# One float32 product for the router's rows and logits, and pools whose long matmul operands begin at multiples of 512 bytes

## The chip, the core and the metric

The kernel runs on one core of a Trainium2 chip. The metric is the device time of one execution in microseconds (us); three runs of the kernel before gave 4136.3, 4138.6 and 4139.27 us, median 4138.6 us. Engines are named as in the profile: PE (matrix products; PEld is its loading of the stationary operand), ACT, DVE, POOL, and SP, which issues most DMAs. A matmul has a stationary operand (`lhsT`, loaded first) and a moving operand (`rhs`, streamed through).

## The reference

```python
X = rfft(x, axis=1)                                   # x: 8 x 3072 x 256
Yr = Xr @ w_r - Xi @ w_i + b_r;  Yi = Xr @ w_i + Xi @ w_r + b_i
Y = soft_threshold(Yr, 0.01) + 1j * soft_threshold(Yi, 0.01)
x = irfft(Y, n=3072, axis=1).reshape(24576, 256)
h = x @ w_in                                          # 256 x 2048
x = where(h >= 1, h, where(h <= -1, 0, (h + 1)**2 / 4)) @ w_out
logits = x @ w_gate                                   # 256 x 8 experts
e = argmax(logits);  gate = softmax(logits)[e]        # per token
out = gate * (relu(x @ w1[e]) @ w2[e])                # 256 x 1024, 1024 x 256
```

## The kernel before

There are three stages, each bounded by pools of SBUF memory that are opened and closed in turn.

The spectral stage (`spectral`, to about 558 us) does the transform as two small products per batch, mixes with the complex weights (L278), thresholds, and does half of the inverse (L305). The dense stage (`Moe1.run`, about 559 to 2925 us) walks over 48 units of 512 tokens with 16 steps each. A step (u, f) is written out in program order: six products of 512 columns for layer 1 (L664: `win` stationary, `yh` and `yl` moving), the nonlinearity on ACT and DVE (L669 to L671), a split of the result into high and low parts (ACT L678, POOL L679), and six products of 512 columns for layer 2 of the step three back (L689: `wout` stationary, `gh` and `gl` moving). The expert stage (`Moe2.run`, from 2925 us) walks over a list of tiles of 512 ("big", 41 of them), 256 (17) and 128 tokens (4). A big tile has eight steps of six 512-column products (L956: `w1b` stationary, `xh`, `xl` moving) and twelve 256-column products (L987: `hh`, `hl` stationary, `w2b` moving). The weights stand in three buffers each: big tiles alternate between `w1b`/`w2b` 0 and 1, the small tiles use 2 (`buf`).

The products run in float32r on operands split into a high and a low part. A float32r product is one record in the trace. A plain float32 product stands in the trace as two records, called passes here; a transpose is one.

Between the first two stages and the experts lies the router. When the dense stage has finished a unit, `Router.add` copies its output to `xc` (256 channels on partitions by 512 tokens, float32) and queues small jobs; `router.jobs.run(3)` takes three of them, `None` included, per step. Two jobs (`rows`, L515) transpose four 128x128 blocks each, so that tokens stand on partitions; ACT copies them to `rw` (L518). A third (`logits`, L524) makes eight float32 products with only 8 moving columns, the gate weights `wg`, and DVE copies them to `lg` (L526). Every second unit, `route` finds the expert and the gate from `lg`, stores token number and gate in the last two columns of `rw`, writes `rw` to the DRAM array `xs`, and works out each token's slot; the slots are written one indirect DMA per step from POOL's queue (`place`, L595). The experts later fetch slots (L877), rows of `xs` (L913) and weights (L877) with indirect DMAs of the same queue and transpose the rows back (L923).

SBUF tiles follow each other in a pool, each rounded to 32 bytes, so a tile's start follows from the sizes of all before it. In the built program of the kernel before, starts modulo 512 bytes are: `win`, `wout` and `yh`, `yl` 480; `gh`, `gl` 352; `w1b0`, `w2b0` 128; `w1b1`, `w1b2`, `w2b1`, `w2b2` and the experts' `xh`, `xl` 352; `hh`, `hl` 480; in the spectral stage `wh`, `wl`, `i1h`, `i1l` 256, and the moving `zh`, `zl` 384. L278's stationary operands start at many different offsets, because they are windows of 194 columns.

Of the kernel before, what the change touches and what calls it, by code (L numbers as in the profile page):

```python
# [10 lines left out]
F32 = mybir.dt.float32  # L11
# [29 lines left out]
XW = D + 2  # L41
# [134 lines left out]
def spectral(tc, nc, a, P, A_dr, B_dr, NB, side, room):  # L176
# [11 lines left out]
    f1 = const.tile([96, 96], F32, name="f1")  # L188
    f1h = const.tile([96, 96], F32R, name="f1h")
    f1l = const.tile([96, 96], F32R, name="f1l")  # L190
# [5 lines left out]
    bias = const.tile([128, 3, D], F32, name="bias")  # L196

# [290 lines left out]
class Router:  # L488


    def __init__(self, tc, nc, a, K, sb, xs_dr, slots):
        self.tc, self.nc, self.K, self.sb, self.xs_dr, self.slots = tc, nc, K, sb, xs_dr, slots
        self.wg = sb.tile([128, 2, NE], F32, name="wg", bufs=1)
        self.open = {}
        self.jobs, self.moves, self.hold = Jobs(), deque(), False
        nc.gpsimd.dma_start(self.wg, a["moe2_w_gate"].rearrange("(c p) e -> p c e", p=128))

    def add(self, u, n, psum):

        sb, nc = self.sb, self.nc  # L500
        k = u % n
        if k == 0:
            self.open[u] = (sb.tile([128, 8, NE], F32, tag="lg", name="lg"),
                            sb.tile([128, 8, XW], F32, tag="rw", name="rw"))
        lg, rw = self.open[u - k]
        xc = sb.tile([128, 2, TT], F32, tag="xc", name="xc")
        nc.scalar.activation(xc, psum, AF.Copy)

        def rows(h):

            p = self.rank_tile()
            for c in range(2):
                for dc in range(2):
                    o = (2 * h + c) * 128
                    nc.tensor.transpose(p[:, (2 * c + dc) * 128:(2 * c + dc + 1) * 128], xc[:, dc, o:o + 128],  # L515
                                        self.K["ident"])
            t = 4 * k + 2 * h
            nc.scalar.activation(rw[:, t:t + 2, 0:D], p.rearrange("p (c d) -> p c d", c=2), AF.Copy)  # L518

        def logits():  # L520
            p = self.rank_tile()
            for c in range(4):
                for dc in range(2):
                    nc.tensor.matmul(p[:, c * NE:(c + 1) * NE], lhsT=xc[:, dc, c * 128:(c + 1) * 128],  # L524
                                     rhs=self.wg[:, dc, :], start=(c == 0 and dc == 0), stop=(c == 3 and dc == 1))
            nc.vector.tensor_copy(out=lg[:, 4 * k:4 * k + 4, :],  # L526
                                  in_=p[:, 0:4 * NE].rearrange("p (c e) -> p c e", c=4))
        self.jobs.add(None, None, None, partial(rows, 0), None, None, partial(rows, 1), None, None, logits, None, None)
        if k == n - 1:
            self.open.pop(u - k)  # L530
            self.jobs.add(self.route(4 * (u - k), 4 * n, lg, rw))

    def route(self, c0, T, lg, rw):
        tc, sb, K = self.tc, self.sb, self.K
        v, sc, pe, gp, sp = self.nc.vector, self.nc.scalar, self.nc.tensor, self.nc.gpsimd, self.nc.sync
        lg, rw = lg[:, 0:T, :], rw[:, 0:T, :]
# [35 lines left out]
        v.reciprocal(out=rw[:, :, D + 1], in_=sm)  # L572
        v.tensor_copy(out=rw[:, :, D].bitcast(I32), in_=ids[:, 0, c0:c0 + T])
# [146 lines left out]
class Moe2:  # L720


    def __init__(self, tc, nc, K, sb, xs_dr, slots, w_dr, out):
        self.tc, self.nc, self.K, self.pre, self.xs_dr, self.slots = tc, nc, K, sb, xs_dr, slots
        self.w_dr, self.out = w_dr, out
        self.w1b = [sb.tile([128, 2, 2, FE], F32R, name="w1b0")]
# [95 lines left out]
    def listing(self, sb, tag, n, num, start, per, back, sure):  # L822
# [5 lines left out]
        def t2(name, dt=F32):  # L828
            return sb.tile([128, n], dt, name=f"{name}_{tag}", bufs=1)
        tt, et, cs, wf, si, wi = t2("tt"), t2("et"), t2("cs"), t2("wf"), t2("si", I32), t2("wi", I32)  # L830
        b3 = sb.tile([128, n, NE], F32, name=f"b3_{tag}", bufs=1)
        last = sb.tile([128, 1], F32, name=f"last_{tag}", bufs=1)
# [85 lines left out]
    def turn(self, t, dc):  # L918
        r, C = self.xr[t], self.chunks(t)
        n = C * 128  # L920
        p = self.ps.tile([128, 512], F32, tag="px", name="px")
        for c in range(C):
            self.nc.tensor.transpose(p[:, c * 128:(c + 1) * 128], r[:, c, dc * 128:(dc + 1) * 128], self.K["ident"])  # L923
        if dc == 0:
            self.xt[t] = (self.sb.tile([128, 2, 512], F32R, tag="xh", name="xh"),
                          self.sb.tile([128, 2, 512], F32R, tag="xl", name="xl"))
        xh, xl = self.xt[t]
        v = self.nc.vector
        self.nc.scalar.activation(xh[:, dc, :n], p[:, :n], AF.Copy)  # L929
        v.tensor_tensor(out=xl[:, dc, :n], in0=p[:, :n], in1=xh[:, dc, :n].bitcast(F32), op=ALU.subtract)  # L930
        if dc == 1:
            o = self.sb.tile([128, 4], I32, tag="oi", name="oi", bufs=4)
            v.tensor_tensor(out=o[:, :C], in0=r[:, :C, D].bitcast(I32), in1=self.ix.pop(t)[2], op=ALU.add)
            self.oi[t] = o
# [57 lines left out]
    def finish(self, t):  # L992
# [4 lines left out]
        for c in range(C):  # L997
            w = r[:, c, D + 1:D + 2]
# [63 lines left out]
def body(tc, a, out, NB=8):  # L1062
# [39 lines left out]
    with tc.manual_schedule():  # L1102
# [10 lines left out]
        def side(s, pool):  # L1113
# [87 lines left out]
```

## Time and profile before

| | |
|---|---|
| median of three runs | 4138.6 us |
| profiled execution: its own time | 4134.41 us |
| its span of engine work | 4132.6 us |
| PE busy | 4100.5 us, 99% |
| DVE, ACT, POOL busy | 53%, 44%, 43% |
| granted TensorE clock, mean | 0.997 of 2.4 GHz |

A PE group's busy time counts matmuls that overlap each other in the pipeline, so the mean of one (401 ns for 512 columns) is longer than the distance between two starts. What a matmul costs on a busy PE is read from that distance, in the timeline.

### The profile page before, as it was taken

What the parts mean: (1) busy time and instruction counts of PE and PEld (TensorE: products, weight loads), DVE (VectorE), ACT (ScalarE), POOL (GpSimd) and SP (SyncE); (2) the same over time, 40 slices, a digit from 0 to 9 for tenths busy, and PEclk for the clock granted to TensorE, in tenths of its full rate; (3) what the DMA queues carried; (4) which work ended last, traced back from release to release, by engine and by line L of the source; (5) the groups of instructions that cost most, each with busy time, mean ns of one, the idle gap of its engine ahead of it and who ended that gap; (6) DMA issues with size and microseconds to landing.
All of it is one profiled execution on the core that took longest, in us unless ns stands there. A gap on an engine that the chain in (4) does not pass through costs nothing.

```text
span 4132.6 us, 61734 instructions
## 1 busy us (share of the span) xinstructions
PE 4100.5 (99%) x23596; PEld 3564.1 (86%) x23596; DVE 2196.6 (53%) x4082; ACT 1817.9 (44%) x3266; POOL 1794.2 (43%) x1590
## 2 busy tenths in 40 slices
PE   8999999999999999999999999999999999999999
PEld 6999988888888888888888888888889899999998
DVE  6999965555555555555555555555533333333333
ACT  5666544444444444444444444444322322232232
POOL 1000024444445454444454555556455545445453
PEclk9999999999999999999999999999999999999999
DMA  8767512211211221222112210002223321113222
GB/s 263 220 212 215 174 49 48 57 48 45 54 50 50 48 52 47 51 49 49 50 50 56 58 31 22 22 21 62 68 88 108 102 85 46 48 43 130 89 82 74
DMA packets 204344, 321.79 MB, mean 78 GB/s; under 512 B 43284, under 2 KB 167090, under 8 KB 200976
## 3 DMA queue, kind: packets, MB, share of 16 engines
q1 hardware_dynamic: 157968, 213.09, 18.6%
q0 software_dynamic: 46080, 104.76, 8.2%
q8 instruction: 185, 3.03, 0.4%
q14 instruction: 111, 0.91, 0.1%
HBM read 392.10 MB, written 136.61 MB: 128 GB/s over the span
## 4 chain that ended last, share of the span: by engine, by line
PE 97%; DMA 1%; DVE 1%; issue 1%; POOL 0%; ACT 0%; SPq 0%; POOLq 0%; ACTq 0%; DVEq 0%
PE po L689 26%; PE pl L664 26%; PE po L987 13%; PE pl L956 13%; PE pmx L278 6%; PE pi L649 3%; PE pf L225 2%; PE prk L524 2%; PE pf L246 2%; PE pi L305 2%; PE px L923 1%; PE prk L515 1%; DMA A<-ao 1%; DMA xr<-xs,gi 0%; DMA at<-A 0%
## 5 line engine op out<-in xcount | busy, mean ns | idle before, releaser
L679 POOL TENSOR_TENSOR gl<-g,gh 128x512 fp32r<-128x512 f32 x768 | 992.6, 1292 | 1125.4 <-ACT gh L678 1078.9
L670 DVE SCALAR_TENSOR_TENSOR q<-q 128x512 f32<-128x512 f32 x768 | 532.3, 693 | 864.5 <-ACT q L669 862.5
L669 ACT ACTIVATE q<-pl,half 128x512 f32<-128x512 f32 x768 | 527.7, 687 | 1027.8 <-PE pl L664 1027.3
L664 PE MATMUL pl<-yh,win 128*128 128x512 f32 x3072 | 857.8, 401 | 0.9 <-DVE g L671 0.9
L689 PE MATMUL po<-gh,wout 128*128 128x512 f32 x3072 | 835.4, 393 | 0.0
L689 PEld LDWEIGHTS po<-gh,wout 128*128 128x128 f32 x3072 | 576.2, 188 | 125.7
L664 PEld LDWEIGHTS pl<-yh,win 128*128 128x128 f32 x3072 | 556.4, 188 | 113.7 <-DVE g L671 1.8
L961 DVE SCALAR_TENSOR_TENSOR hl<-pl,hh 128x512 fp32r<-128x512 f32 x396 | 273.7, 691 | 576.9 <-ACT hh L960 574.9
L671 DVE TENSOR_TENSOR g<-pl,q 128x512 f32<-128x512 f32 x768 | 531.3, 692 | 83.2 <-DVE q L670 4.6
L960 ACT ACTIVATE hh<-pl 128x512 fp32r<-128x512 f32 x396 | 237.3, 599 | 639.8 <-PE pl L956 625.5
L689 PE MATMUL po<-gl,wout 128*128 128x512 f32 x1536 | 483.6, 395 | 0.0
L678 ACT ACTIVATE gh<-g 128x512 fp32r<-128x512 f32 x768 | 477.2, 621 | 4.2 <-DVE g L671 4.2
L664 PE MATMUL pl<-yl,win 128*128 128x512 f32 x1536 | 474.3, 390 | 0.0
L987 PEld LDWEIGHTS po<-w2b,hh 128*128 128x128 f32 x3232 | 434.9, 188 | 29.1
L956 PE MATMUL pl<-xh,w1b 128*128 128x512 f32 (+1 forms) x1856 | 454.8, 367 | 0.7 <-ACT xh L929 0.7
L987 PE MATMUL po<-w2b,hh 128*128 128x256 f32 x3232 | 449.4, 281 | 0.0
L689 PEld LDWEIGHTS po<-gl,wout 128*128 128x128 f32 x1536 | 288.3, 188 | 69.9
L664 PEld LDWEIGHTS pl<-yl,win 128*128 128x128 f32 x1536 | 288.4, 188 | 65.1
L956 PEld LDWEIGHTS pl<-xh,w1b 128*128 128x128 f32 x1856 | 297.8, 189 | 30.5 <-ACT xh L929 1.3
L1005 POOL DMA_INDIRECT out<-y,oi x202 | 205.2, 1016 | 210.7 <-ACT y L1000 162.7
L956 PE MATMUL pl<-xl,w1b 128*128 128x512 f32 (+1 forms) x928 | 260.0, 361 | 0.0
L987 PE MATMUL po<-w2b,hl 128*128 128x256 f32 x1616 | 258.3, 282 | 0.8 <-DVE hl L961 0.8
(260 smaller groups left out, 4760.1 us busy)
## 6 DMA issues: line engine op xcount, KB each, us to landing
xs<-rw SPq DMA_DIRECT2D x24, 1032.0 KB, 6.5
A<-ao SPq DMA_DIRECT2D x64, 384.0 KB, 4.2
at<-A SPq DMA_DIRECT2D x96, 256.0 KB, 3.7
B<-bo SPq DMA_DIRECT2D x96, 256.0 KB, 2.7
xt<-in_x SPq DMA_DIRECT2D x56, 384.0 KB, 4.8
ws<-in_moe_w SPq DMA_DIRECT2D x128, 128.0 KB, 3.3
w_dr<-wsh SPq DMA_DIRECT2D x128, 128.0 KB, 1.8
w_dr<-wsl SPq DMA_DIRECT2D x128, 128.0 KB, 2.5
```

What stands on the lines that cost most here:

```text
L278: pe.matmul(p[:, gi, :], lhsT=l, rhs=r, start=(i == 0), stop=(i == 11))
L664: self.nc.tensor.matmul(p, lhsT=w[:, kc, f * 128:(f + 1) * 128], rhs=y[:, kc, :], start=(i == 0), stop=(i == 5))
L669: self.nc.scalar.activation(q, p, AF.Relu, bias=self.K["half"], scale=0.5)
L670: v.scalar_tensor_tensor(out=q, in0=q, scalar=1.0, in1=q, op0=ALU.min, op1=ALU.mult)
L671: v.tensor_tensor(out=g, in0=p, in1=q, op=ALU.max)
L678: self.nc.scalar.activation(gh, g, AF.Copy)
L679: self.nc.gpsimd.tensor_tensor(out=gl, in0=g, in1=gh.bitcast(F32), op=ALU.subtract)
L689: self.nc.tensor.matmul(self.po[u][:, dc, :], lhsT=w[:, f, dc * 128:(dc + 1) * 128], rhs=g, start=(f == 0 and i == 0), stop=(f == 15 and i ...
L956: self.nc.tensor.matmul(p[:, h * n:(h + 1) * n], lhsT=w[:, part, kc, k * 128:(k + 1) * 128], rhs=x[:, kc, :n], start=(i == 0), stop=(i == 5))
L960: self.nc.scalar.activation(hh, p, AF.Relu)
L961: self.nc.vector.scalar_tensor_tensor(out=hl, in0=p, scalar=0.0, in1=hh.bitcast(F32), op0=ALU.max, op1=ALU.subtract)
L987: self.nc.tensor.matmul(self.po[t][:, c, :], lhsT=h[:, k * n + c * 128:k * n + (c + 1) * 128], rhs=w[:, part, m * f + k, :], start=(first ...
```

## The change

`Router.add` now makes rows and logits together. `wg` becomes two blocks of 136 columns: for channels 0 to 127 the identity followed by the gate weights, for channels 128 to 255 the gate weights followed by the identity. Per 128 tokens two float32 products of 136 moving columns write one PSUM tile, the second starting at column 128: rows of the first half stand in columns 0 to 127, the sum of both logits in 128 to 135, rows of the second half in 136 to 263. One ACT copy moves all 264 columns to `rw`, so `lg` and its DVE copy are gone, a row of `xs` has 266 floats in place of 258, and the jobs of a unit cover four steps in place of three. The gate weights and the identity are loaded by four DMAs on POOL's queue in place of one.

```diff
+XL = 128
+XW = D + NE + 2
...
-        self.wg = sb.tile([128, 2, NE], F32, name="wg", bufs=1)
+        self.wg = sb.tile([128, 2, XL + NE], F32, name="wg", bufs=1)
+        sb.tile([128, 136], F32, name="pad_r", bufs=1)
...
-        nc.gpsimd.dma_start(self.wg, a["moe2_w_gate"].rearrange("(c p) e -> p c e", p=128))
+        for dc in range(2):
+            nc.gpsimd.dma_start(self.wg[:, dc, dc * NE:dc * NE + 128], a["c_sq"][:, 0, :])
+            nc.gpsimd.dma_start(self.wg[:, dc, XL * (1 - dc):XL * (1 - dc) + NE], a["moe2_w_gate"][dc * 128:(dc + 1) * 128, :])
...
-        def rows(h):
-            p = self.rank_tile()
-            for c in range(2):
-                for dc in range(2):
-                    o = (2 * h + c) * 128
-                    nc.tensor.transpose(p[:, (2 * c + dc) * 128:(2 * c + dc + 1) * 128], xc[:, dc, o:o + 128],
-                                        self.K["ident"])
...
-        def logits():
...
-        self.jobs.add(None, None, None, partial(rows, 0), None, None, partial(rows, 1), None, None, logits, None, None)
+        def rows(c):
             p = self.rank_tile()
+            for dc in range(2):
+                nc.tensor.matmul(p[:, dc * XL:dc * XL + XL + NE], lhsT=xc[:, dc, c * 128:(c + 1) * 128],
+                                 rhs=self.wg[:, dc, :], start=(dc == 0), stop=(dc == 1), skip_group_check=True)
+            nc.scalar.activation(rw[:, 4 * k + c, 0:D + NE], p[:, 0:D + NE], AF.Copy)
+        self.jobs.add(None, None, None)
+        for c in range(4):
+            self.jobs.add(partial(rows, c), None, None)
...
+        lg = rw[:, :, XL:XL + NE]
...
-            self.nc.tensor.transpose(p[:, c * 128:(c + 1) * 128], r[:, c, dc * 128:(dc + 1) * 128], self.K["ident"])
+            self.nc.tensor.transpose(p[:, c * 128:(c + 1) * 128], r[:, c, dc * (XL + NE):dc * (XL + NE) + 128], self.K["ident"])
```

The rest moves memory. Three unused tiles are inserted as spacers, the forward table's `f1` moves from the constants to a rotating buffer, the scratch tiles of the expert lists become one tile (for the early list one of the three `xr` buffers), and the small `oi` tiles move to another pool.

```diff
-    f1 = const.tile([96, 96], F32, name="f1")
+    f1 = xp.tile([96, 96], F32, tag="cv_s", name="f1", bufs=2)
...
+        sb.tile([128, 96], F32, name="pad_p")
...
+        if tag == "early":
+            z = sb.tile([128, 4, XW], F32, tag="xr", name="list", bufs=3).rearrange("p c d -> p (c d)")
...
-            o = self.sb.tile([128, 4], I32, tag="oi", name="oi", bufs=4)
+            o = self.pre.tile([128, 4], I32, tag="oi", name="oi", bufs=4)
...
+                wp.tile([128, 120], F32, name="pad_w")
```

In the built program of the changed kernel `win`, `wout`, `yh`, `yl`, `gh`, `gl`, all `w1b` and `w2b`, the experts' `xh`, `xl`, `hh`, `hl` and the spectral `zh`, `zl` start at 0 modulo 512. `wh`, `wl`, `i1h`, `i1l` start at 128.

On PE, in the dense stage around the first unit's router jobs (`prk` is the router's PSUM tile), the kernel before has:

```order
L689 MATMUL po<-gl,wout_815 128x512 x2
L515 MATMUL prk<-ident,xc 128x128 x4
L664 MATMUL pl_7577<-yh,win_813 128x512 x2
...
L515 MATMUL prk<-ident,xc 128x128 x4
...
L524 MATMUL prk<-wg,xc 128x8 x8
L664 MATMUL pl_7637<-yh,win_813 128x512 x2
```

On the same engine, at the same place, the changed kernel has:

```order
L684 MATMUL po<-gl,wout_815 128x512 x2
L517 MATMUL prk<-wg,xc 128x136 x2
L659 MATMUL pl_7580<-yh,win_813 128x512 x2
...
L517 MATMUL prk<-wg,xc 128x136 x2
...
L517 MATMUL prk<-wg,xc 128x136 x2
...
L517 MATMUL prk<-wg,xc 128x136 x2
L659 MATMUL pl_7664<-yh,win_813 128x512 x2
```

Between two router jobs stand one step's twelve products, in both. Eight transposes and eight products of 8 columns in three steps have become eight products of 136 columns in four; the order of the long products is as it was.

On POOL, at the start of the expert stage (`slots<-ids` is `place`, `si_t<-slots` the fetch of a tile's slots, `xr<-xs` that of its rows), the kernel before has:

```order
L913 DMA xr<-xs,gi 128x258 x4
L604 MEMSET spare 1x1
L595 DMA slots<-ids,r_si 197120x1
L877 DMA w1b_7133<-w_dr,wi_early 128x4096
L1005 DMA out<-y,oi 24576x256
L877 DMA w2b_7134<-w_dr,wi_early 128x4096
L1005 DMA out<-y,oi 24576x256
L604 MEMSET spare 1x1
L595 DMA slots<-ids,r_si 197120x1
L877 DMA si_t<-slots,si_early 128x4
```

On POOL at the same place the changed kernel has:

```order
L913 DMA xr<-xs,gi 128x266 x4
L877 DMA w1b_7139<-w_dr,wi_early 128x4096
L1005 DMA out<-y,oi 24576x256
L877 DMA w2b_7140<-w_dr,wi_early 128x4096
L1005 DMA out<-y,oi 24576x256
L599 MEMSET spare 1x1
L590 DMA slots<-ids,r_si 197120x1
L877 DMA si_t<-slots,si_early 128x4
```

The last pair's eight slot writes begin one step later, so that one of them stands ahead of the fetch of the next tile's slots where two stood.

## Rows read from the trace of the kernel before

**Rows 1.** The page, busy time and share of each engine.

```profile
PE 4100.5 (99%) x23596; PEld 3564.1 (86%) x23596; DVE 2196.6 (53%) x4082; ACT 1817.9 (44%) x3266; POOL 1794.2 (43%) x1590
```

**Rows 2.** Busy time by stretch: start:end, length, engines, clock, DMA share, GB/s.

```profile
1000.00:2000.00 1000.00, 1000.00 (x4817) 828.33 (x4816) 552.77 (x988) 488.39 (x870) 499.72 (x408) 1.00 0.21 50
3500.00:4000.00 500.00, 500.00 (x3480) 465.75 (x3479) 174.58 (x349) 148.39 (x267) 249.83 (x251) 1.00 0.25 80
```

**Rows 3.** What PE waited for from 560 us on: total, times, longest.

```profile
PE px L923 <- DMA xr<-xs,gi: 1.2, 1, 1.2
PE pl L664 <- DVE g L671: 0.9, 1, 0.9
```

**Rows 4.** Timeline of PE, one unit's router jobs: start, length, group.

```profile
2092.55 1.08 PE L664 MATMUL pl<-yh,win 128*128 128x512 f32 x4
...
2095.67 1.17 PE L664 MATMUL pl<-yh,win 128*128 128x512 f32 x4
...
2098.54 0.60 PE L515 MATMUL prk<-ident,xc 128*128 128x128 f32 x4
2098.89 1.17 PE L664 MATMUL pl<-yh,win 128*128 128x512 f32 x4
...
2101.76 1.85 PE L524 MATMUL prk<-wg,xc 128*128 128x8 f32 x16
2103.46 1.17 PE L664 MATMUL pl<-yh,win 128*128 128x512 f32 x4
...
2106.32 1.08 PE L664 MATMUL pl<-yh,win 128*128 128x512 f32 x4
...
2107.70 1.09 PE L689 MATMUL po<-gh,wout 128*128 128x512 f32 x4
...
2109.09 1.08 PE L664 MATMUL pl<-yh,win 128*128 128x512 f32 x4
```

**Rows 5.** Timeline of PEld, a float32 product of 128 columns.

```profile
542.27 0.97 PEld L246 LDWEIGHTS pf<-f,at 128*128 128x128 f32 x8
...
543.16 0.54 PEld L278 LDWEIGHTS pmx<-wh,xh 128*128 128x128 f32 x4
```

**Rows 6.** Groups by line: count, busy us, mean ns of one, idle before.

```profile
L524 PE MATMUL prk<-wg,xc 128*128 128x8 f32 x768 | 88.6, 251 | 0.0
L518 ACT ACTIVATE rw<-prk 128x512 f32<-128x512 f32 x96 | 57.7, 601 | 59.5 <-PE prk L515 59.5
L515 PE MATMUL prk<-ident,xc 128*128 128x128 f32 x384 | 57.4, 272 | 0.0
L1000 ACT ACTIVATE y<-po,xr 128x256 f32<-128x256 f32 x99 | 42.5, 472 | 49.6 <-PE po L987 48.7 <-DMA w1b<-w_dr,wi_early 0.8
```

**Rows 7.** Timeline of PE, steps of two big tiles, buffers 1 and 0.

```profile
3012.10 1.08 PE L956 MATMUL pl<-xh,w1b 128*128 128x512 f32 x4
...
3013.47 1.13 PE L987 MATMUL po<-w2b,hh 128*128 128x256 f32 x8
...
3014.92 1.09 PE L956 MATMUL pl<-xh,w1b 128*128 128x512 f32 x4
...
3027.11 1.10 PE L956 MATMUL pl<-xh,w1b 128*128 128x512 f32 x4
...
3028.50 1.12 PE L987 MATMUL po<-w2b,hh 128*128 128x256 f32 x8
...
3029.93 1.10 PE L956 MATMUL pl<-xh,w1b 128*128 128x512 f32 x4
```

**Rows 8.** Timeline of PE, the 24 products of one L278 pair.

```profile
302.37 0.63 PE L278 MATMUL pmx<-wh,xh 128*128 128x256 f32 x4
...
305.20 0.28 PE L305 MATMUL pi<-zh,i1h 128*128 128x256 f32 x1
```

**Rows 9.** Timeline of POOL between the spectral and the dense stage.

```profile
550.86 0.75 POOL L496 DMA_DIRECT2D wg<-in_moe_w_gate  x1 [48.11 <-DVE vv L282]
563.28 1.28 POOL L679 TENSOR_TENSOR gl<-g,gh 128x512 fp32r<-128x512 f32 x1 [11.68 <-ACT gh L678]
```

More of the change, by code (lines that the diff above doesn't have):

```diff
@@ L196, in spectral @@
     bias = const.tile([128, 3, D], F32, name="bias")
+    f1h = const.tile([96, 96], F32R, name="f1h")
+    f1l = const.tile([96, 96], F32R, name="f1l")
     xt, x2, at, st_a, st_b, xs, vs, zs, i1f = {}, {}, {}, {}, {}, {}, {}, {}, {}
@@ L502, in add @@
         if k == 0:
-            self.open[u] = (sb.tile([128, 8, NE], F32, tag="lg", name="lg"),
-                            sb.tile([128, 8, XW], F32, tag="rw", name="rw"))
-        lg, rw = self.open[u - k]
+            self.open[u] = sb.tile([128, 8, XW], F32, tag="rw", name="rw")
+        rw = self.open[u - k]
         xc = sb.tile([128, 2, TT], F32, tag="xc", name="xc")
         nc.scalar.activation(xc, psum, AF.Copy)
-        def rows(h):
+        def rows(c):
             p = self.rank_tile()
-            for c in range(2):
-                for dc in range(2):
-                    o = (2 * h + c) * 128
-                    nc.tensor.transpose(p[:, (2 * c + dc) * 128:(2 * c + dc + 1) * 128], xc[:, dc, o:o + 128],
-                                        self.K["ident"])
-            t = 4 * k + 2 * h
-            nc.scalar.activation(rw[:, t:t + 2, 0:D], p.rearrange("p (c d) -> p c d", c=2), AF.Copy)
@@ L520, in logits @@
-        def logits():
-            p = self.rank_tile()
[L522 to L527, printed above, removed]
@@ L529, in add, with route @@
+        for c in range(4):
+            self.jobs.add(partial(rows, c), None, None)
         if k == n - 1:
             self.open.pop(u - k)
-            self.jobs.add(self.route(4 * (u - k), 4 * n, lg, rw))
-    def route(self, c0, T, lg, rw):
+            self.jobs.add(self.route(4 * (u - k), 4 * n, rw))
+    def route(self, c0, T, rw):
         tc, sb, K = self.tc, self.sb, self.K
         v, sc, pe, gp, sp = self.nc.vector, self.nc.scalar, self.nc.tensor, self.nc.gpsimd, self.nc.sync
-        lg, rw = lg[:, 0:T, :], rw[:, 0:T, :]
+        rw = rw[:, 0:T, :]
+        lg = rw[:, :, XL:XL + NE]
@@ L571, in route @@
         v.tensor_scalar(out=sm, in0=sm, scalar1=1e-9, scalar2=None, op0=ALU.add)
-        v.reciprocal(out=rw[:, :, D + 1], in_=sm)
-        v.tensor_copy(out=rw[:, :, D].bitcast(I32), in_=ids[:, 0, c0:c0 + T])
+        v.reciprocal(out=rw[:, :, XW - 1], in_=sm)
+        v.tensor_copy(out=rw[:, :, XW - 2].bitcast(I32), in_=ids[:, 0, c0:c0 + T])
         sp.dma_start(self.xs_dr.rearrange("(t p) d -> p t d", p=128)[:, c0:c0 + T, :], rw)
@@ L826, in listing @@
         pn = tl[:, NBIG:NBIG + 1]
[L828 to L832, printed above, removed]
+        if tag == "early":
+            z = sb.tile([128, 4, XW], F32, tag="xr", name="list", bufs=3).rearrange("p c d -> p (c d)")
+        else:
+            z = sb.tile([128, (4 + NE) * n + 1], F32, name=f"list_{tag}", bufs=1)
+        tt, et, cs, wf = (z[:, i * n:(i + 1) * n] for i in range(4))
+        b3 = z[:, 4 * n:(4 + NE) * n].rearrange("p (n e) -> p n e", e=NE)
+        last = z[:, (4 + NE) * n:(4 + NE) * n + 1]
+        si, wi = (sb.tile([128, n], I32, name=f"{i}_{tag}", bufs=1) for i in ("si", "wi"))
         io = tl[:, 0:n]
@@ L931, in turn @@
         if dc == 1:
-            o = self.sb.tile([128, 4], I32, tag="oi", name="oi", bufs=4)
-            v.tensor_tensor(out=o[:, :C], in0=r[:, :C, D].bitcast(I32), in1=self.ix.pop(t)[2], op=ALU.add)
+            o = self.pre.tile([128, 4], I32, tag="oi", name="oi", bufs=4)
+            v.tensor_tensor(out=o[:, :C], in0=r[:, :C, XW - 2].bitcast(I32), in1=self.ix.pop(t)[2], op=ALU.add)
             self.oi[t] = o
@@ L997, in finish @@
         for c in range(C):
-            w = r[:, c, D + 1:D + 2]
+            w = r[:, c, XW - 1:XW]
             if c < C // 2:
```

3 lines of the change are left out of this document (removed).

## The prediction

> **What bounds the kernel now.** I read the page's busy times first: PE is busy for 99% of the span, no other engine for more than 53% [rows 1]. An average can hide stages, so the table by stretch came next: in the dense stage and in the expert stage PE is busy for every microsecond of a stretch, at a granted clock of 1.00 (the 2.4 GHz level), while ACT, DVE and POOL have half of their time or more free and the DMA engines three quarters [rows 2]. The waits confirm it: after 560 us PE's longest single waits are 1.2 us for a gather of token rows and 0.9 us for DVE [rows 3]. So from 560 us on the time is the sum of the distances between PE's starts, and a change is worth what it does to these. The timeline of PE gives them, since starts and not lengths count there.
>
> Two distances matter. A plain dense step, twelve products of 512 columns, lasts 2109.09 - 2106.32 = 2.77 us, of which L664's six take 1.38 and L689's six 1.39 [rows 4]. That is 0.231 us a product. And a unit's router jobs: from 2092.55 to 2106.32 there are four steps, two with four transposes, one with the logits, and one that only carries a late start over (2.86 us). They last 13.77 us in place of 4 x 2.77 = 11.08, so the router costs 2.69 us of PE time a unit, 129 us over 48 units [rows 4].
>
> **Router, removed and added.** Taken apart, a job of four transposes costs 2098.89 - 2095.67 - 2.77 = 0.45 us, 0.112 a transpose. The sixteen passes of the logits cost 2103.46 - 2101.76 = 1.70 us plus the 0.09 by which the next step is longer, again 0.112 a pass [rows 4]; the counts, 384 transposes and 768 passes, are the trace's [rows 6]. A pass with 8 moving columns thus costs what a transpose of 128 does: the load of the stationary operand sets the distance and not the columns. A float32 product of 128 columns says the same: its eight loads start (543.16 - 542.27)/8 = 0.111 us apart [rows 5].
>
> The new form needs 8 products, so 16 passes a unit, of 136 columns. No row shows 136. From below, the load still hides them: 0.111. From above, 128 columns may already fill the 0.111, and 136 would take 0.111 x 136/128 = 0.118. I take the middle, 0.114, as both ends are near. Then a unit costs 16 x 0.114 = 1.82 us and saves 0.87, over 48 units **42 us** (38 to 44). All of it lies on the path, as PE has nothing else to wait for.
>
> What the router adds elsewhere is covered by PE's own time. ACT copies four tiles of 264 columns, at about 0.47 us each by the 256-column eviction from PSUM, in place of two at 0.60 [rows 6]: 0.7 us more a unit of 16 steps, on an engine that is idle for half of its time [rows 2]. Without that cover it would be 33 us. Each copy stands ahead of one `q` activation, as two copies a unit do now without making PE wait, and the next user of a PSUM buffer comes a step later. DVE loses 48 small copies and reads the logits with a larger stride; it is not waited for. POOL issues four loads for `wg`, some 0.75 us each, ending near 554 us, ahead of its next work at 563 [rows 9]. Rows of `xs` grow by 3%, on DMA engines with three quarters free. A unit's jobs take four steps, so `route` and the slot writes start one step later; on POOL's queue the last pair's first slot write is passed by two weight fetches, and one such write, not two, stands ahead of the fetch of the next tile's slots. The gather behind it is the one that PE waited 1.2 us for [rows 3]. I allow 1.2 us less to 3 us more, and count nothing. `f1`, `oi` and the lists only move; `f1` gets an unused buffer, and the early list leaves its `xr` buffer long before the gather that follows.
>
> **Starts at multiples of 512 bytes.** This is the uncertain term. The trace has no such operands, so I compare rows that do the same work at other starts. In the expert stage odd big tiles use buffer 1, where stationary `w1b1` and moving `xh` both start at 352 modulo 512: L956's six take 3013.47 - 3012.10 = 1.37 us. Even tiles use `w1b0` at 128 against the same `xh`: 1.39 us. L987 has its moving `w2b` at 352 in odd tiles, 1.45 us for twelve, and at 128 in even ones, 1.43 [rows 7]. L278, whose moving operands start at 256 and whose stationary ones are scattered, needs 2.83 us for 24 products of 256 columns, 1.415 for twelve [rows 8]. So addresses do matter, by 1 to 2.5%. Equal offsets of both operands look better for 512 columns (L664, both at 480, 1.38; L689, 352 against 480, 1.39). A multiple of 128 for the moving operand looks better for 256 columns.
>
> After the change both operands start at 0. I let L689 go to the 1.37 of the equal pair: 0.02 x 768 steps = 15 us. L956 in the even tiles likewise: 0.02 x 168 = 3 us. L987 in the odd tiles goes to 1.43: 0.02 x 160 = 3 us. Together **21 us**. The bounds are the fastest and the slowest of these rows. At the fastest everywhere, a dense step is 12 x 1.37/6 = 2.74 us, 23 us less in 768 steps, L956 is 3 us less, and L987's 404 groups drop from about 1.435 to 1.415, 8 us less: 34 us gained. At the slowest everywhere, L664 at 1.39 costs 8 us, the odd tiles' L956 3 us, the even tiles' L987 at 1.45 4 us: 15 us lost. The value is nearer the fast end because the equal pairs are the fast ones.
>
> A rule speaks against this term. The rows show operands that start at 480 and 352, multiples of 32 but not of 64, and still differ by 1.5% at most for 512 columns [rows 4, 7]. The Trainium skill, page "SBUF — State Buffer", section "Door 1: The DMA port swizzle (why `[64,N]` ≈ `[32,N]`)", says that SBUF has lines of 16 bytes and that what costs is crossing to a new line without using it. By that rule every old start was on a line already and the layout gives nothing; by the rows it gives 21 us. The 1.45 against 1.43 between two buffers speaks against the rule as the whole story, so I keep it as a rival.
>
> **The sum.** The profiled execution took 4134.4 us; 4134.4 - 42 - 21 = 4071.4. The median of the three runs is 4.2 us above that execution, and I add these: **4076 us**. About 0.2%, 8 us, is what a measurement of this kernel can tell from no change.
>
> **Rivals.**
>
> *The starts don't matter.* The differences between buffers then come from something else that alternates with the tiles, and only the router counts: 4138.6 - 42 = 4097 us. For it: L278, with stationary operands at dozens of offsets, is as fast as anything else of 256 columns [rows 8]. Against it: rows 7. Chance 19%.
>
> *The starts matter more than rows can show.* None of the rows has both operands at a multiple of 512, and there could be a step there. If all long products lose as much as the slowest group stands above the fastest, 1.45 against 1.415 or 2.5%, that is 2.5% of 768 x 2.77 + 328 x 1.39 + 404 x 1.43 = 3161 us, so 79 us: 4138.6 - 42 - 79 = 4018 us. Against it: moving operands at a multiple of 256 are only 1% faster than those at a multiple of 128 [rows 7, 8]. The Trainium skill, page "TensorE: Matmul & The Clock Gate", section "Back-to-back issue gap", has 512 columns at N/2.4 + 2.5, 216 ns, at the high clock; the trace has 231 here, and by the page there would be 6% to win, near 190 us. No row says that the starts are what is in the way. Chance 12%.
>
> *The router's product is not cheap.* If a pass of 136 columns cost 2.69/16 = 0.168 us, the gain would be gone: 4138.6 - 21 = 4118 us. This needs 1.5 times the pass of 128 columns for 6% more columns. Chance 5%.
>
> *Equal phases collide (slower).* With every start at the same place modulo 512, the load of the next stationary operand and the moving stream that it overlaps touch the same part of a 512-byte block in each of the long products. If that stretches them by the 2.5% between the slowest and the fastest group, it costs the 79 us from above: 4138.6 - 42 + 79 = 4176 us. It decides from 42 us on, 1.3% of the long products, 3 ns on 231. Against it: where both start at the same offset now, the rows are the fastest (L664 1.38, odd L956 1.37) [rows 4, 7]. Chance 4%.
>
> **How the numbers follow.** Forecast 60%, with its own range 4060 to 4100; starts without effect 19%; large effect 12%; dear router product 5%; collision 4%. The range 4005 to 4112 leaves out the deeper part of the large effect, most of the dear product and the collision, less than 2 in 10. Faster by over 0.2% are the first three and the greater part of the fourth less a rest for a mild collision, 0.91; within 0.2% that rest, 0.05; slower the collision, 0.04.
>
> **What would show it.** A router job should add 4 x 0.114 = 0.46 us to a dense step, in four steps a unit; 0.67 would mean the dear product. A plain step should go from 2.77 to about 2.75 us: at 2.77 the starts don't matter, at 2.70 or less they matter more than rows show, at 2.80 or more they collide. L956 should take 1.37 us in even and odd tiles alike, and L987 1.43. PE should stay at 99% with the clock at 1.00, and its waits after 560 us below 6 us. The forecast is wrong if PE waits for the router's PSUM tiles, for ACT, or for a gather by more than that, or if the plain step moves by more than 0.04 us either way.

## The result and the profile after

The changed kernel takes 4077.6 us (median of four runs, 4072.5 to 4079.7) where the kernel before takes 4137.5 (four runs, 4133.4 to 4139.3): a ratio of 0.9855, 95% interval 0.9838 to 0.9872, so 60 us less. The forecast was 4076 us. The profiled execution took 4072.5 us, with a span of 4070.7. In the changed kernel L664 is L659, L689 is L684, and the router's products are L517.

The page's first line, and the table by stretch of the changed kernel, columns as in [rows 2]:

```profile
PE 4038.7 (99%) x23212; PEld 3532.5 (87%) x23212; DVE 2223.6 (55%) x4034; ACT 1835.7 (45%) x3362; POOL 1836.3 (45%) x1593
```

```profile
1000.00:2000.00 1000.00, 1000.00 (x4783) 836.10 (x4782) 578.24 (x993) 507.48 (x936) 525.41 (x412) 1.00 0.20 52
3500.00:4000.00 500.00, 500.00 (x3463) 466.20 (x3463) 174.14 (x346) 147.40 (x265) 249.09 (x251) 1.00 0.26 85
```

PE is still busy for every microsecond of both stretches, so the distances of its starts are still the time. What PE waited for from 555 us on, to be read against [rows 3]:

```profile
PE po L987 <- DVE hl L961: 1.3, 1, 1.3
PE ph L969 <- DVE xl L930: 1.3, 4, 0.3
PE pl L659 <- DVE g L666: 1.1, 2, 0.9
PE pl L956 <- ACT xh L929: 0.7, 1, 0.7
```

4.4 us in all, and the wait for a gather of 1.2 us is gone. The timeline of PE over one unit's router jobs, the counterpart of [rows 4]:

```profile
2096.43 1.07 PE L659 MATMUL pl<-yh,win 128*128 128x512 f32 x4
...
2097.79 1.07 PE L684 MATMUL po<-gh,wout 128*128 128x512 f32 x4
...
2099.15 1.07 PE L659 MATMUL pl<-yh,win 128*128 128x512 f32 x4
...
2101.87 0.62 PE L517 MATMUL prk<-wg,xc 128*128 128x136 f32 x4
2102.25 1.18 PE L659 MATMUL pl<-yh,win 128*128 128x512 f32 x4
...
2105.49 1.18 PE L659 MATMUL pl<-yh,win 128*128 128x512 f32 x4
...
2114.83 1.07 PE L659 MATMUL pl<-yh,win 128*128 128x512 f32 x4
```

A plain step now lasts 2099.15 - 2096.43 = 2.72 us, 1.36 for either six; it was 2.77, with 1.38 and 1.39. The unit's router costs 2114.83 - 2099.15 - 5 x 2.72 = 2.08 us; it was 2.69 by the rows and 2.71 by the medians of all units. A step that follows a job and holds one takes 2105.49 - 2102.25 = 3.24, so a job costs 0.52 us.

The chain of waits in the expert stage, start and length of each group, from two big tiles that follow each other:

```profile
2974.17 1.39 PE pl L956 x6
2975.55 1.43 PE po L987 x12
...
2989.15 1.39 PE pl L956 x6
2990.54 1.43 PE po L987 x12
```

The two buffers look alike now, and a pair of groups takes 2.82 us, as it did in either of them in [rows 7]. But [rows 7] shows one step of each, and its last L987 isn't the even tile's: layer 2 runs one step behind layer 1, so the twelve at 3028.50 are still the odd tile's last. The chain of waits in the kernel before, two steps of the same odd tile, and then the even tile's first twelve:

```profile
3009.42 1.40 PE pl L956 x6
3010.82 1.44 PE po L987 x12
3012.26 1.38 PE pl L956 x6
3013.64 1.45 PE po L987 x12
...
3030.09 1.39 PE pl L956 x6
3031.48 1.41 PE po L987 x12
```

Over all steps of the big tiles that hold nothing else, the medians of the kernel before are 1.391 (L956) and 1.440 us (L987) in odd tiles, 1.393 and 1.412 in even ones. A pair took 2.829 us in the mean in odd tiles and 2.809 in even ones (the five pairs over 2.9 us left out); now it takes 2.820 in both.

Where the time went, from PE's first product on, by the start of the first product of each stage and of PE's last: up to the dense stage 556.7 us before and 555.0 after, the dense stage 2370.0 and 2309.5, the expert stage 1195.5 and 1195.6. All of the gain is in the dense stage: the 1.7 us of the first stage are less than the 4 us by which two profiles of the kernel before differ there (the other, of the last run below, has 560.6). By medians of its steps over the units: 16 steps a unit at 0.047 less are 0.047 x 768 = 36 us; the router's excess over plain steps fell from 2.71 to 2.08 us a unit, 30 us; and the excess of the inverse jobs (L644) and of the steps behind them rose from 2.42 to 2.51, 4 us back.

### The profile page after: what moved, and what is told of

Its sections match the earlier page's. It is cut to its first block, busy times and chain, and to the rows that moved or that the text cites. A ratio compares the mean times of both kernels' runs of the same rounds, so it can differ in the third digit from the quotient of the medians.

```text
span 4070.7 us, 61014 instructions
## 1 busy us (share of the span) xinstructions
PE 4038.7 (99%) x23212; PEld 3532.5 (87%) x23212; DVE 2223.6 (55%) x4034; ACT 1835.7 (45%) x3362; POOL 1836.3 (45%) x1593
## 4 chain that ended last, share of the span: by engine, by line
PE 95%; DVE 3%; DMA 1%; issue 1%; ACT 1%; POOL 0%; SPq 0%; DVEq 0%; ACTq 0%; POOLq 0%
PE pl L659 26%; PE po L684 26%; PE po L987 14%; PE pl L956 13%; PE pmx L280 5%; PE pi L644 3%; PE prk L517 2%; PE pf L227 2%; PE pf L248 2%; PE pi L307 1%; PE px L923 1%; DMA A<-ao 1%; DVE zl L298 0%; DVE vv L284 0%; DVE xl L257 0%
## 5 line engine op out<-in xcount | busy, mean ns | idle before, releaser
L665 DVE SCALAR_TENSOR_TENSOR q<-q 128x512 f32<-128x512 f32 x768 | 545.6, 710 | 822.7 <-ACT q L664 819.0
L664 ACT ACTIVATE q<-pl,half 128x512 f32<-128x512 f32 x768 | 529.6, 690 | 890.1 <-PE pl L659 887.8
L659 PE MATMUL pl<-yh,win 128*128 128x512 f32 x3072 | 858.4, 401 | 1.2 <-DVE g L666 1.1
L684 PE MATMUL po<-gh,wout 128*128 128x512 f32 x3072 | 825.9, 390 | 0.0
L684 PEld LDWEIGHTS po<-gh,wout 128*128 128x128 f32 x3072 | 576.8, 188 | 123.9
L659 PEld LDWEIGHTS pl<-yh,win 128*128 128x128 f32 x3072 | 552.6, 188 | 99.7 <-DVE g L666 3.1
L960 ACT ACTIVATE hh<-pl 128x512 fp32r<-128x512 f32 x396 | 237.0, 599 | 636.6 <-PE pl L956 619.2
L684 PE MATMUL po<-gl,wout 128*128 128x512 f32 x1536 | 474.2, 390 | 0.0
L659 PE MATMUL pl<-yl,win 128*128 128x512 f32 x1536 | 474.1, 390 | 0.0
L987 PEld LDWEIGHTS po<-w2b,hh 128*128 128x128 f32 x3232 | 436.3, 190 | 27.4
L956 PE MATMUL pl<-xh,w1b 128*128 128x512 f32 (+1 forms) x1856 | 456.1, 367 | 0.7 <-ACT xh L929 0.7
L987 PE MATMUL po<-w2b,hh 128*128 128x256 f32 x3232 | 451.0, 282 | 0.0
L659 PEld LDWEIGHTS pl<-yl,win 128*128 128x128 f32 x1536 | 288.3, 188 | 64.8
L684 PEld LDWEIGHTS po<-gl,wout 128*128 128x128 f32 x1536 | 288.4, 188 | 62.2 <-POOL gl L674 0.2
L956 PEld LDWEIGHTS pl<-xh,w1b 128*128 128x128 f32 x1856 | 299.0, 190 | 30.3 <-ACT xh L929 1.3
L987 PE MATMUL po<-w2b,hl 128*128 128x256 f32 x1616 | 259.8, 283 | 1.3 <-DVE hl L961 1.3
L956 PE MATMUL pl<-xl,w1b 128*128 128x512 f32 (+1 forms) x928 | 258.2, 359 | 0.0
```

Source lines behind the costliest of these rows:

```text
L659: self.nc.tensor.matmul(p, lhsT=w[:, kc, f * 128:(f + 1) * 128], rhs=y[:, kc, :], start=(i == 0), stop=(i == 5))
L664: self.nc.scalar.activation(q, p, AF.Relu, bias=self.K["half"], scale=0.5)
L665: v.scalar_tensor_tensor(out=q, in0=q, scalar=1.0, in1=q, op0=ALU.min, op1=ALU.mult)
L684: self.nc.tensor.matmul(self.po[u][:, dc, :], lhsT=w[:, f, dc * 128:(dc + 1) * 128], rhs=g, start=(f == 0 and i == 0), stop=(f == 15 and i ...
L956: self.nc.tensor.matmul(p[:, h * n:(h + 1) * n], lhsT=w[:, part, kc, k * 128:(k + 1) * 128], rhs=x[:, kc, :n], start=(i == 0), stop=(i == 5))
L960: self.nc.scalar.activation(hh, p, AF.Relu)
```

## The experiments

All start from the kernel before or the changed kernel. The first four runs (the two parts, the first dense scan, the first expert scan) were on a chip on which the kernel before takes 4136 us; all others but the last on two chips on which it takes 4280 us. A fence of the edits shows the lines that matter, with `...` where lines are left out. Ratios are always to the kernel before on the same chip.

**The router alone**, with the operands' starts as before (a pad keeps them):

```diff
+        self.wg = sb.tile([128, 2, XL + NE], F32, name="wg", bufs=1)
+        sb.tile([128, 32], F32, name="pad_r", bufs=1)
...
-        self.jobs.add(None, None, None, partial(rows, 0), None, None, partial(rows, 1), None, None, logits, None, None)
+        self.jobs.add(None, None, None)
+        for c in range(4):
+            self.jobs.add(partial(rows, c), None, None)
```

> The router change alone; every operand of the long products starts where it started before (gh at 352, wout at 480 modulo 512 and so on). Theory 'phase' (a product that follows short products runs off a steady rhythm, and only the new layout has such a rhythm to lose): plain dense step stays at 2.77 us, a router job adds 4 x 0.116 = 0.46 us, a unit's router 1.85 to 1.90 in place of 2.71, so 39 us less, about 4098. Rival 'dear product' (the pass of 136 columns is what made the router cost 2.08 us a unit in the changed kernel): the job adds 0.52 us here too, 30 us less, about 4107.

Measured: 4097.5 us against 4135.9, ratio 0.9906 (0.9889 to 0.9922), 38.5 us less. PE's timeline of this kernel, where the jobs are L515 and the layer 1 products L657:

```profile
2120.03 1.08 PE L657 MATMUL pl<-yh,win 128*128 128x512 f32 x4
...
2122.80 0.62 PE L515 MATMUL prk<-wg,xc 128*128 128x136 f32 x4
...
2135.72 1.08 PE L657 MATMUL pl<-yh,win 128*128 128x512 f32 x4
```

Five steps, from 2120.03 to 2135.72, hold the unit's four jobs and last 15.69 us, 1.85 above 5 x 2.767. The same sixteen passes that cost 2.08 in the changed kernel cost 1.85 here. So a pass isn't dear in itself: inside a job the passes start 115 to 116 ns apart in both kernels, and 16 x 0.1156 is 1.85. What is added in the changed kernel lies in the long products behind a job. From the second to the twelfth of them, their starts are 231.3 ns apart in the mean there, where a plain step has 226.7; here they are 230.6 apart, which is the pace of this kernel's plain step too.

**The layout alone**, with the old router:

```diff
-    f1 = const.tile([96, 96], F32, name="f1")
+    f1 = xp.tile([96, 96], F32, tag="cv_s", name="f1", bufs=2)
...
+        sb.tile([128, 40], F32, name="pad_r", bufs=1)
...
+        sb.tile([128, 96], F32, name="pad_p")
...
-            o = self.sb.tile([128, 4], I32, tag="oi", name="oi", bufs=4)
+            o = self.pre.tile([128, 4], I32, tag="oi", name="oi", bufs=4)
...
+                wp.tile([128, 120], F32, name="pad_w")
```

> The layout alone, with the old router. All theories: plain dense step 2.72 us as in the changed kernel, L987's twelve 1.43, since the layout is what they hang on. Theory 'phase': each of the three router jobs and two inverse jobs of a unit now also breaks the rhythm of the step behind it (0.04 to 0.06 us each), so of 768 x 0.047 = 36 us some 20 to 26 are left, about 4112 to 4117; the old router costs about 2.85 us a unit here. Rival 'no interplay': old router 2.71 as before, 33 us less, about 4105. If plain steps stay at 2.77 the layout was not the cause at all.

Measured: 4112.2 us, ratio 0.9944 (0.9928 to 0.9961), 23.7 us less. The chain of waits in the dense stage (layer 1 is L665, layer 2 L690):

```profile
2113.67 1.36 PE pl L665 x6
2115.03 1.36 PE po L690 x6
```

Plain steps are at 2.72 as in the changed kernel, which would be 36 us, but the old router's excess rose from 2.71 to 2.83 us a unit, and with the inverse jobs 9 us of the dense stage were given back (2370.0 to 2343.3). The two parts done alone add up to 62.2 us, the whole gave 59.9.

**A scan of the moving operand's start in the dense stage**: `gh` and `gl` of each unit at one of eight starts, `wout` at 0.

```diff
+        o = (0, 256, 32, 128, 16, 64, 480, 352)[u % 8] // 4
-        gh = self.sb.tile([128, TT], ...)
+        gh = self.sb.tile([128, TT + 128], ...)[:, o:o + TT]
```

> The changed kernel with the moving operands gh and gl of L684 started at 0, 256, 32, 128, 16, 64, 480 or 352 bytes modulo 512, by unit (unit number modulo 8); the stationary wout stays at 0, L659 at 0 and 0. One buffer fewer for xc makes room. Plain steps without router or inverse jobs, L684's six products: theory 'multiple of 512' 1.36 us only in units at 0, 1.38 to 1.39 in the others; theory 'multiple of 64' 1.36 at 0, 64, 128, 256 and 1.38 or more at 16, 32, 352, 480; theory 'equal offsets of both operands' the same as 'multiple of 512' here (told apart by a later run with both at 480).

Measured: 4100.8 us (one run). The chain of waits, a unit with `gh` at 0, then one at 128 (layer 2 is L685):

```profile
1764.27 1.36 PE po L685 x6
1765.63 1.36 PE pl L659 x6
...
1909.51 1.39 PE po L685 x6
1910.90 1.38 PE pl L659 x6
```

Medians of all undisturbed sixes: 1.360 at 0 and 256, 1.384 at 64, 1.389 at 16, 1.392 at 128, 1.402 to 1.405 at 32, 480 and 352. So 512 isn't the number, nor is 64. And at 128 L659, whose own operands haven't moved, is slowed with its neighbour, to a median of 1.375 us, which is what L664 took in the kernel before.

**The same scan with the other operand moved**: `win`, `wout`, `yh` and `yl` 384 bytes past a multiple of 512 (the smaller pad moves them up).

```diff
-                wp.tile([128, 120], F32, name="pad_w")
+                wp.tile([128, 24], F32, name="pad_w")
...
+        o = (0, 256, 32, 128, 384, 64, 480, 352)[u % 8] // 4
```

> The changed kernel with the dense stage's weights and yh, yl beginning 384 bytes past a multiple of 512, and gh, gl of each unit at one of eight starts (0, 256, 32, 128, 384, 64, 480 and 352 bytes past a multiple of 512). Theory, both operands have to begin at a multiple of 256 bytes: no pair does, so no unit's six of L684 take 1.360 us, all take 1.38 to 1.41, L659's six (384 beside 384) 1.37 to 1.39, the plain step is 2.75 to 2.79, and the time 4095 to 4115 us. Rival, equal starts of the two operands are what counts: L659's six stay at 1.360 and so do L684's of the units at 384, all others longer, 4085 to 4095 us. Rival, only the moving operand's start counts: L684 at 1.360 in the units at 0 and 256 and at 1.38 to 1.40 elsewhere, L659 longer, 4090 to 4110 us.

Measured: 4241.7 us (one run). The chain of waits, a unit with `gh` at 0, then one at 128:

```profile
1764.93 1.39 PE po L685 x6
1766.32 1.38 PE pl L659 x6
...
1910.70 1.36 PE po L685 x6
1912.06 1.36 PE pl L659 x6
```

The two starts have changed places: 128 is fast and 0 slow. Units at 384 and 128 took 1.360 us, those at 0 and 256 1.392. All three expectations failed: the theory of multiples, since nothing here begins at one; equal starts, since 128 beside 384 isn't equal; the moving operand alone, since 0 and 256 are slow. What fits is the difference of the two starts modulo 256 bytes: at 0 the products settle to 1.360. The kernel before agrees: L664 had 480 beside 480, L689 480 beside 352, a difference of 128, and 1.392.

**The difference, put to the test** with a third start, 480, for the weights, and eight new ones for `gh`:

```diff
-                wp.tile([128, 120], F32, name="pad_w")
...
+        o = (480, 0, 224, 96, 352, 160, 32, 416)[u % 8] // 4
```

> The changed kernel with the dense stage's weights and yh, yl beginning 480 bytes past a multiple of 512 and gh, gl of each unit at one of eight starts (480, 0, 224, 96, 352, 160, 32, 416). Theory, formed on the two scans before: what counts is the difference of the two operands' starts modulo 256 bytes. The scans give for L684's six 1.360 us at a difference of 0, 1.384 at 192, 1.392 at 128, 1.400 at 64 and 1.402 at 224; so here 1.360 in the units at 480 and at 224 (difference 0), 1.384 at 32, 1.392 at 96 and 352, 1.400 at 160 and 416, 1.402 at 0, and L659's six (480 beside 480) at 1.360 in the units where L684's are. Rival, starts have to be multiples of 128 bytes as well as equal modulo 256: no unit at 1.360, L659 at 1.37 to 1.39.

Measured: 4242.4 us (one run). The chain of waits, units with `gh` at 0, 224 and 96:

```profile
1809.04 1.40 PE po L685 x6
1810.44 1.39 PE pl L659 x6
...
1859.34 1.36 PE pl L659 x6
1860.70 1.36 PE po L685 x6
...
1906.09 1.39 PE po L685 x6
1907.48 1.38 PE pl L659 x6
```

Medians: 1.360 at 480 and 224, 1.384 at 32, 1.392 at 96 and 352, 1.400 at 160 and 416, 1.402 at 0. All eight came out as forecast, to the nanosecond. Neither operand needs to begin at a multiple of 64 or more: 480 and 224 are multiples of 32 alone. In every unit at 1.360 the difference of the two is a multiple of 256, and in no other.

**Scans in the expert stage**: `hh`, `hl` of each pair of big tiles at one of eight starts, with `w2b` 1 and 2 moved to 128 in the first scan and left at 0 in the second.

```diff
+        return (0, 256, 32, 128, 16, 64, 480, 352)[j // 2 % 8] // 4 if kind == "big" else 0
...
+        o = self.at(t)
-        hh = self.sb.tile([128, 512], ...)
+        hh = self.sb.tile([128, 640], ...)[:, o:o + 512]
...
+        sb.tile([128, 32], F32, name="pad_x", bufs=1)
```

> The changed kernel with the stationary operands hh and hl of L987 started at 0, 256, 32, 128, 16, 64, 480 or 352 modulo 512 by pair of big tiles, and the moving w2b1, w2b2 at 128 (w2b0 at 0). Twelve products of 256 columns: theory 'rhythm' (at equal phases 256 columns fall to 120 ns, 1.43 us for twelve, and off them they are shorter on average): 1.43 at 0 and 0, about 1.41 at most other pairs, among them 128 against 480, the old pair of w2b0. Rival 'multiples are best': 1.43 at 0, 64, 128, 256 and 1.44 or more at 16, 32, 352, 480. Total time within 10 us of the changed kernel.

> The changed kernel with hh and hl of the large expert tiles at one of eight starts by the pair of tiles (480, 496, 448, 416, 384, 320, 224 and 192 bytes past a multiple of 512), w2b at a multiple of 512 as it is. Theory, 256-column products settle into a slow rhythm when both operands begin at multiples of 64 bytes: L987's twelve take 1.415 to 1.44 us at 448, 384, 320 and 192 and 1.40 to 1.42 at 480, 496, 416 and 224, 4066 to 4072 us. Rival, how far the start lies past the multiple of 512 decides and not what it divides by: the sum falls evenly from 1.44 at 192 to 1.40 at 480 and 496. Rival, nothing but the PSUM bank or the buffer decides: 1.43 at all eight, 4072 us.

Measured: 4072.5 and 4231.6 us (one run each). The chain of waits of the second, tiles with `hh` at 384 and at 224 (L956 is L960 and L987 is L993 here):

```profile
3703.84 1.39 PE pl L960 x6
3705.23 1.45 PE po L993 x12
...
3809.12 1.39 PE pl L960 x6
3810.51 1.40 PE po L993 x12
```

Products of 256 columns have a best difference of their own. Medians of twelve, stationary start less moving start modulo 256: 1.43 to 1.44 at 0, 1.44 to 1.45 at 128, 1.41 at 64 and 192, 1.40 at 224. So 1.43 is close to the longest of them, and the layout put L987 there. Of the first scan's expectations the rival failed at 64 and 16 (1.41 and 1.42 us, where it had 1.43 and 1.44 or more), and the rhythm failed at `hh` 128 beside `w2b` 0 and at 0 and 256 beside 128 (1.44 to 1.45, longer than the 1.43 at equal starts). Of the second scan's expectations, the multiples of 64 failed at 416 (1.430, no multiple, and slow), the distance at 192 (1.411, where 1.44 was due), and the rival without an effect everywhere. At a difference of 192 about one twelve in six took 1.36 in the second scan.

**More and fewer groups of router passes**: the sixteen passes as eight jobs of two, and as two jobs of eight.

```diff
-        for c in range(4):
-            self.jobs.add(partial(rows, c), None, None)
+        for c in range(4):
+            for dc in range(2):
+                self.jobs.add(partial(rows, c, dc), None, None)
```

or

```diff
-        for c in range(4):
-            self.jobs.add(partial(rows, c), None, None)
+        for c in range(0, 4, 2):
+            self.jobs.add(lambda c=c: (rows(c), rows(c + 1)), *[None] * 5)
```

> The changed kernel with the same 16 router passes a unit given out as eight jobs of two passes in eight steps, not as four jobs of four. Theory, behind each group of short products the long ones run out of rhythm and lose 0.055 us: four more groups a unit, of which one and a third fall into steps that hold an inverse job already, so 2.67 x 0.055 x 48 = 7 us more, 4076 to 4083 us; a step with a two-pass job takes 2.72 + 0.23 + 0.055 = 3.0 us. Rival, a router job costs what its passes take and no more than that: 2.95 us a step, 4072 to 4074 us.

> The changed kernel with the same 16 router passes a unit given out as two jobs of eight passes, not as four of four. Theory, each group of short products costs the long ones behind it 0.055 us: two groups fewer a unit, 2 x 0.055 x 48 = 5.3 us less, 4065 to 4069 us. Rival, a job costs its passes and no more: 4071 to 4074 us. A second rival, that the two PSUM tiles that a job of eight holds make the inverse jobs or TensorE wait: 4074 to 4080 us, with waits on ACT in the steps that hold a job.

Measured, on one chip: 4231.9 us for eight jobs, ratio 0.9880 (0.9864 to 0.9895), and 4215.6 for two, 0.9839 (0.9824 to 0.9854). The expected times in microseconds were for a chip on which the kernel before takes 4136 us; only the differences can be compared. The dense stage took 2318.6 and 2301.7 us, against 2310.8 for the changed kernel on the other chip of 4280 us (the last run but one): 7.8 us more, where 7 was forecast, and 9.1 less, where 5.3 was. PE's timeline with eight jobs (L520) and with two (L517):

```profile
2108.90 1.18 PE L664 MATMUL pl<-yh,win 128*128 128x512 f32 x4
...
2111.77 0.39 PE L520 MATMUL prk<-wg,xc 128*128 128x136 f32 x2
2111.91 1.18 PE L664 MATMUL pl<-yh,win 128*128 128x512 f32 x4
```

```profile
2100.47 1.07 PE L659 MATMUL pl<-yh,win 128*128 128x512 f32 x4
...
2103.19 1.09 PE L517 MATMUL prk<-wg,xc 128*128 128x136 f32 x8
2104.03 1.16 PE L659 MATMUL pl<-yh,win 128*128 128x512 f32 x4
...
2106.84 1.07 PE L659 MATMUL pl<-yh,win 128*128 128x512 f32 x4
```

At 0.1156 us a pass (the starts inside a job), two passes are 0.231 us and cost 3.01 - 2.72 = 0.29; four are 0.462 and cost 0.52; eight are 0.925 and cost 6.37 - 2 x 2.72 = 0.93. So a group of two or four passes takes 0.06 us from the long products behind it, a group of eight next to nothing. The starts show it one by one: behind a group of eight the long products are 226.7 ns apart from the second on, behind a group of two 230.5 and behind one of four 231.3. Why the length of the group matters is open. PE's waits in the whole dense stage were 1.2 and 0.9 us, so the rival that has PE wait for PSUM fell.

**A version from what was found**, and the changed kernel again beside it: two router jobs a unit, and `hh`, `hl` 192 bytes past a multiple of 256.

```diff
+        for c in range(0, 4, 2):
+            self.jobs.add(lambda c=c: (rows(c), rows(c + 1)), *[None] * 5)
...
-        hh = self.sb.tile([128, 512], ...)
+        hh = self.sb.tile([128, 576], ...)[:, 48:560]
```

> The changed kernel with two router jobs of eight passes a unit in place of four of four, and with hh and hl beginning 192 bytes past a multiple of 256 (w2b at a multiple of 512). From the steps of the runs before: the dense stage 2309.5 - 7.8 = 2301.7 us, and in the expert stage L956's six and L987's twelve together 2.780 to 2.788 us and not 2.820, 0.035 x 404 = 14 us less, so 22 us less than the changed kernel beside it and a ratio to the kernel before of 0.978 to 0.982. Rival, the shorter twelve come from the mixture of starts in the scan and don't last when all tiles have the same one: the expert stage stays, 8 us less, ratio 0.983 to 0.985.

> The changed kernel as it is, beside the others on the same chip: a ratio to the kernel before of 0.984 to 0.987 and a dense stage of 2309 to 2312 us, by every theory.

Measured: 4205.3 us, ratio 0.9831 (0.9816 to 0.9845), beside 4227.8, ratio 0.9885 (0.9869 to 0.9900). So it beats both, by 22.5 us over the changed kernel (4198 to 4211 us against 4224 to 4231). Its dense stage took 2301.5 us against 2310.8, its expert stage 1330.0 against 1342.0; 9 and 14 were forecast, 9 and 12 came. The chain of waits in a big tile of the new version:

```profile
3005.37 1.37 PE pl L956 x6
3006.74 1.41 PE po L987 x12
3008.15 1.37 PE pl L956 x6
```

A pair of groups takes 2.78 us, not 2.82. L956's six fell from 1.39 to 1.37 in it although only the operands of L987 beside it were moved. Both ratios missed their ranges. That of the new version lies in its rival's range, but the rival had the expert stage unchanged, and it was 12 us shorter than in the changed kernel on the same chip; what is missing is missing in the changed kernel's ratio too. The changed kernel's dense stage was what it had been in its first profile, but its expert stage took 1342 us and not 1196, and it gained 52.6 us over the kernel before and not 60. ACT waited there for what the profile can't name:

```profile
ACT hh L960 <- remote: 178.0, 47, 11.6
ACT xh L929 <- remote: 24.4, 5, 5.1
```

No such wait stands in the first profile of the changed kernel. PE itself waited 102 us in that stage here, 49 of them put down to ACT and 52 to no cause that the profile shows, and its granted clock was 0.97 in the mean, where it was 1.00.

**The kernel before, for its profile there.** The source is unchanged.

> The kernel before as it is, for its profile beside the last runs of the changed kernel, whose expert stage took 1342 us there against 1195.6 in the first profile, with 200 us of ACT's waits in it put down to no engine of the core. Theory, those waits belong to the chip and come to any of these kernels: dense stage 2369 to 2372 us, expert stage 1335 to 1350 us with 150 to 220 us of such waits. Rival, the changed kernel brings them: expert stage 1195 to 1200 us and the dense stage longer.

Measured: 4137.8 us, dense stage 2370.7, expert stage 1194.4. It ran on yet another chip, one on which the kernel before takes 4138 us, so its profile decides nothing between the two expectations. What is known is that beside the runs with the waits the kernel before took 4280 us too, 143 more than elsewhere: the longer time isn't the change's doing. In which stage it falls for the kernel before, why the change gained 7 us less, and what ACT waits for stay open.

## Why the prediction was right, and where not

The total was right to 2 us, and what bounds the kernel was right too: PE never became the one that waits. Done alone, the parts gave 38.5 and 23.7 us where 42 and 21 were forecast. Inside the whole kernel the split is another: the router gave 30 us, the dense layout 32 where 15 were counted, and the expert layout nothing where 6 were. The errors nearly cancel, and that the total came within 2 us is luck in that measure.

- **The router's 42 us were 30 in the changed kernel.** The pass was sized well: 0.1156 us, inside 0.111 to 0.118. The step that failed is "a router job should add 4 x 0.114 = 0.46 us": it adds 0.52. The prediction let the long products behind a job go on as in a plain step. At 2.77 us a step they do (1.85 a unit is what the passes alone take). Once they run at 226.7 ns, a group of four passes puts them back to 231 for a step, which takes 0.06 us a job. The trace of before couldn't show this, as its products run at 231 anyway.
- **The layout's 21 us were 36 in the plain steps, less 4 at the inverse jobs.** The step that failed is the one that left L664 at 1.38, since its two operands had equal starts already, and took 1.37 for L689. Both go to 1.360. L664 had been held up by L689 beside it: in the first dense scan a difference of 128 in layer 2 alone brought layer 1 back to 1.375. The prediction said that the forecast is wrong if the plain step moves by more than 0.04 us: it moved by 0.047, and by that test this term was wrong. The reason it gave, that pairs with equal offsets take the least time, was the right one, and the runs made it sharper: equal modulo 256.
- **The expert stage gave nothing where 6 us were counted.** The step that failed is the reading of [rows 7]. Its 1.43 us for L987 "in even tiles" belongs to an odd tile; the even tiles' own twelves took 1.41. So L987 at 1.43 us in both buffers, as forecast, is luck: it is 0.01 less than before in odd tiles and 0.02 more in even ones. The six of L956 at 1.37 were one step of two that alternate; with both operands at 352 they took 1.391 in the median, against 1.393 at different starts, and they stand at 1.39 now. That L956 runs at 1.37 beside an L987 that was moved shows that it too is held up by its neighbour. In the mean a pair gained 0.009 us in odd tiles and lost 0.011 in even ones. The rule that a multiple of 128 is better for the moving operand goes with the reading: the second scan, with `w2b` at a multiple of 512, shows 1.40 us for twelve with `hh` at 224 or 480, and 1.45 with `hh` at 384.
- **Covers held.** ACT's copies of 264 columns took 393 ns, not 470, and hid behind PE; the four loads of `wg` ended near 551.2 us; PE's waits stayed below 6 us.
- **The rivals.** "The starts don't matter", which the Trainium skill's page "SBUF — State Buffer" (section "Door 1: The DMA port swizzle (why `[64,N]` ≈ `[32,N]`)") would give by its lines of 16 bytes (an access that crosses to a new line pays, those to the same line don't), fell with the layout alone (0.9944) and with the scans: all starts were multiples of 16, and the sixes still ran from 1.360 to 1.405 us. The larger effect needed 2.5% on all long products; 1.7% came in the plain dense steps and none in the experts. The Trainium skill's page "TensorE: Matmul & The Clock Gate" (section "Back-to-back issue gap") has 216 ns for 512 columns at the high clock, as the gap of an isolated product; the fastest steady spacing in these runs is 226.7. Of the dear product, which would have cost 42 us, 12 came, and as a loss behind the jobs and not in the pass. The collision of equal phases is the reverse of what 512 columns do; for 256 columns a difference of 0 does take longer than most others.

## What to carry to other kernels

Where PE is the bound, read the distances of its starts, and look up the starts of both operands of the long products: their difference modulo 256 bytes set the distance here, and its best value was another for 512 columns than for 256, so pad by what a scan inside one kernel shows and not to a round number. Put short products between long ones in few groups: two groups of eight cost 0.2 us a unit less than four of four. And when two edits touch the same engine, time each alone before adding their gains, because the sum can be right with both terms wrong.

## What the runs showed of the hardware

Float32r products of 512 columns, granted clock 1.00, six of them, by the difference of the stationary start less the moving one modulo 256 bytes, from the three scans: 1.360 us at 0, 1.384 at 192, 1.389 at 240, 1.392 at 128, 1.398 at 96, 1.400 at 64, 1.402 at 32 and 224, 1.405 at 160. Starts that gave the same difference gave the same six in different scans, whatever the start itself. A float32 pass of 136 columns took 0.1156 us. And the kernel before took 4137 us on some chips and 4280 on others; on the latter the changed kernel had its dense stage the same to 0.1% (2309.5 and 2310.8 us) and its expert stage 146 us longer, with 202 us of ACT's waits in it put down to no engine of the core.
